# A new order, bank plan, engine choice and transposition form for an RWKV-7 plus mixer kernel on one core

## The chip, the core and the metric

The kernel runs on one core of a Trainium2 chip. The core's engines work side by side, each through its own list of instructions in order: TensorE (PE, with its weight loads PEld), VectorE (DVE), ScalarE (ACT), GpSimd (POOL) and SyncE (SP), which here only issues DMAs. An instruction waits on semaphores for what it needs, and everything behind it on its engine waits with it. The metric is the device time of one execution in microseconds (us); the median of the runs counts.

## The reference

Two parts, one behind the other. The first is a recurrence over 768 tokens for 4 batches of 8 heads with 40 x 40 states; the second mixes its output `x` (768 x 320 in each batch) over tokens and channels.

```python
for t in range(S):
    y[:, :, t] = np.einsum('bhd,bhde->bhe', rt, state)
    Sa = np.einsum('bhde,bhe->bhd', state, at)
    state = state * wt[:, :, None, :] - np.einsum('bhd,bhe->bhde', Sa, bt) \
            + np.einsum('bhd,bhe->bhde', vt, kt)
...
theta = x @ w_theta
zr, zi = x * np.cos(theta), x * np.sin(theta)
y = w_tok_r @ zr + w_tok_i @ zi
u = x + y
out = u + np.maximum(u @ w_ch, 0.0)
```

## The kernel before

The tokens are cut into chunks of 128: six to a batch, 24 in all, numbered i = 0 to 23. In a chunk the recurrence is turned into matrix products; from chunk to chunk only a state (`gt`) is handed on.

For each chunk these steps are planned, each an entry with a fixed number, an engine and a list of what it reads and writes:

- SP loads w, k, b, a, v and r (lines 485 and 501; for the first 8 chunks two chunks at a time). Buffers are few, so a load waits until the last reader of its buffer is done, and the loads behind it on SP wait too.
- `prep`: ScalarE takes the logarithm of w (L529), TensorE sums it, ScalarE takes exponentials (L563, L570, L574); GpSimd multiplies k, b and a with them (`kb` and `ah`, L513) or casts inputs to bf16 (L519). TensorE transposes the results (L434, L443), ScalarE (L472) or VectorE (L476) takes them out of PSUM into `feat`, `kb`, `nuT` and so on.
- `scores` (L716): three products of chunk columns, and a fourth in `readout`. Their 128 x 1024 results are masked on the way out: by VectorE in one instruction (L724), or copied by ScalarE (L726) and then masked by GpSimd with a select (L728).
- `recurrence` (x0 L755 and L760, nu L772, gt L793) and `readout` (y L885 and L891), with short evictions on ScalarE (`nx` L766, `nu` L776) and VectorE (`xp` L898).
- `theta` and `sines`: x is transposed (xT), multiplied with w_theta (L850 for the third part of the contraction, L857 for the rest), and ScalarE takes sine and cosine (L923); GpSimd multiplies them with x into `z` (L513).
- `mix_row`: 12 products per chunk with blocks of w_tok (L945), six steps of two; each step needs the `z` of one chunk of the same batch. Then `up` = sum + x on VectorE (L955), its transposition (uT), the channel product with w_ch (L850, L857), `oo` on VectorE (L979) and the store by SP (L982).

The weights come by GpSimd's own queue: w_theta (numbers 52 and 51) and w_ch (53 and 54) in two pieces each (L992), w_tok in six blocks of rows, each with a real and an imaginary half (L1000). A block of w_tok is transposed by TensorE before use. Steps that the prediction names by number: 96 and 97 load the first block of w_tok, 98 transposes it; 305 and 304 load the fifth, 306 transposes it; 363 and 364 load the sixth, 365 transposes it; 400 is the first channel product; 488 is `kb` of chunk 8; 493 and 666 are the casts of r for chunks 8 and 12, 819 that of v for chunk 14.

What sets the order is written out by hand in five tables. `ORDER` lists all 1396 steps; each engine does its own steps in that order. `HOMES` gives each PSUM result one of 8 banks, or a pair of them; a result can't be written before the last reader of the bank's former content is done. `PICK` lists the steps that take their other form:

- a cast on GpSimd instead of ScalarE or the other way round, an eviction on VectorE instead of ScalarE or the other way round;
- scores evicted by ScalarE with a GpSimd select instead of VectorE alone;
- a transposition done whole instead of in halves. Halved, each 128 x 128 block is two transposes of 64 rows, with a pair of banks for the result; whole, it is one transpose of 128 rows, in one bank where it fits.

`WARM` puts filler products of a constant tile (L1048) in front of named steps, as (count, bank). `Plan.thin` drops waits that another wait already implies.

Of the kernel before, what the change touches and what calls it, by code (L numbers as in the profile page):

```python
# [252 lines left out]
def kernel(  # L253
# [800 lines left out]
    for o in plan.order():  # L1054
        if o.idx in WARM:
            fill(*WARM[o.idx])
# [40 lines left out]
```

## Time and profile before

| | |
|---|---|
| median of 3 runs | 200.23 us (198.94 to 202.12) |
| profiled execution | 200.51 us |
| its span, first to last instruction | 197.9 us |
| granted TensorE clock | 0.996 |
| TensorE matmul, instructions | 4064 |
| bytes moved by DMA | 30.96 MB |

The span is what the profile covers; the 2.6 us beyond it are around the program. A view of the profile names a group as line, engine, operation, what is written and read, and its count; L716 is line 716 of the kernel. Busy time of TensorE is modelled from pipelined matmuls, so start-to-start distances are the better price of one.

### The profile page before, as it was taken

The page shows a single profiled execution, that of the slowest core. Times are in us where ns is not written, and L with a number is a line of the kernel's source. Part 1 is how long each engine was busy: PE and PEld are TensorE (multiplying, and loading weights), DVE is VectorE, ACT ScalarE, POOL GpSimd, SP SyncE. Part 2 cuts the span into 40 slices and gives each one's busy share as a digit, 9 for nine tenths or more (in the row PEclk, how much of TensorE's full clock was granted, in tenths as well). Part 3 has the DMA queues.
Part 4 walks back from the last instruction along what each step waited for, and adds up shares of the span by engine and source line. Part 5 has one row for each costly group of instructions (what it writes and reads, how often), then busy time and mean ns, then how long its engine had stood idle before and what let it go on. Part 6 is the DMA issues. An engine that isn't in the chain of part 4 may idle for free.

```text
span 197.9 us, 9187 instructions
## 1 busy us (share of the span) xinstructions
PE 184.9 (93%) x4064; PEld 147.0 (74%) x4064; DVE 158.4 (80%) x263; ACT 161.6 (82%) x304; POOL 144.8 (73%) x173
## 2 busy tenths in 40 slices
PE   7689999999997999999889999999999999999992
PEld 7568789888885768696667778867877777876650
DVE  7689999999999898889779778698885875971451
ACT  3599999999998999996689889999989878865020
POOL 6245576695699889999938997799999579578000
PEclk9999999999999999999999999999999999999998
DMA  5999988996999989989989949897984201000332
GB/s 128 296 275 286 337 202 180 217 177 100 196 157 176 198 138 191 187 136 215 139 143 159 211 139 180 202 158 160 277 146 69 70 11 62 0 3 3 132 123 76
DMA packets 106806, 30.96 MB, mean 156 GB/s; under 512 B 94224, under 2 KB 106768, under 8 KB 106768
## 3 DMA queue, kind: packets, MB, share of 16 engines
q1 hardware_dynamic: 102416, 27.53, 64.6%
q0 software_dynamic: 4352, 2.86, 9.1%
q8 instruction: 31, 0.51, 1.0%
q14 instruction: 7, 0.06, 0.1%
HBM read 29.29 MB, written 3.93 MB: 168 GB/s over the span
## 4 chain that ended last, share of the span: by engine, by line
PE 56%; DMA 15%; POOL 12%; ACT 10%; issue 3%; DVE 1%; SPq 1%; POOLq 0%
PE ps L945 18%; PE ps L716 7%; PE ps L434 6%; PE ps L857 6%; PE ps L443 5%; POOL z L513 3%; DMA raw_v<-in_v_dram 3%; DMA wrow<-in_moe_w_tok_i_dram 3%; PE ps L891 3%; DMA wth<-in_moe_w_theta_dram 3%; DMA raw_w<-in_w_dram 3%; POOL kb L513 3%; DMA raw_r<-in_r_dram 3%; PE ps L850 2%; ACT feat L686 2%
## 5 line engine op out<-in xcount | busy, mean ns | idle before, releaser
L945 PE MATMUL ps<-z,wtok 128*128 128x320 bf16 x288 | 48.7, 299 | 0.0
L724 DVE TENSOR_TENSOR lam<-ps,mask_p 128x1024 bf16<-128x1024 f32 x33 | 40.1, 1219 | 4.8 <-PE ps L716 4.7
L513 POOL TENSOR_TENSOR z<-cs,xp 128x640 bf16<-128x640 f32 x22 | 30.6, 1406 | 3.0 <-ACT cs L923 3.0
L945 PEld LDWEIGHTS <-wtok 128*128 128x128 bf16 x288 | 24.7, 97 | 8.8
L513 POOL TENSOR_TENSOR kb<-raw_kb,ex 128x640 bf16<-128x640 f32 x16 | 22.9, 1433 | 1.4 <-ACT nu L776 1.3
L724 DVE TENSOR_TENSOR phi<-ps,mask_n 128x1024 bf16<-128x1024 f32 x16 | 19.4, 1219 | 4.3 <-PE ps L716 4.1
L716 PEld LDWEIGHTS <-feat 64*128 64x128 bf16 x576 | 17.5, 94 | 6.3 <-issue 3.0
L724 DVE TENSOR_TENSOR psi<-ps,mask_p 128x1024 bf16<-128x1024 f32 x17 | 20.7, 1219 | 0.5 <-PE ps L716 0.3
L728 POOL TENSOR_SCALAR_AFFINE_SELECT lam<-lam 128x1024 bf16<-128x1024 bf16 x15 | 16.4, 1095 | 5.7 <-ACT lam L726 5.7
L716 PE MATMUL ps<-feat 64*128 64x128 bf16 x384 | 18.3, 217 | 0.5 <-DVE feat L666 0.2
L979 DVE SCALAR_TENSOR_TENSOR oo<-ps,up 128x640 f32<-128x640 f32 x11 | 9.1, 823 | 10.7 <-PE ps L857 10.6
L513 POOL TENSOR_TENSOR ah<-raw_a,ex 128x320 bf16<-128x320 f32 x16 | 12.9, 808 | 5.1 <-ACT ex L570 5.0
L726 ACT ACTIVATE lam<-ps 128x1024 bf16<-128x1024 f32 x15 | 15.3, 1029 | 0.4 <-PE ps L716 0.4
L891 PE MATMUL ps<-kb,lam 128*128 128x40 bf16 x384 | 15.6, 180 | 0.0
L472 ACT COPY feat<-ps 128x1024 f32<-128x1024 f32 x14 | 14.3, 1020 | 0.9 <-PE ps L434 0.9
L472 ACT COPY uT<-ps 128x384 f32<-128x384 f32 (+1 forms) x12 | 5.5, 457 | 11.6 <-PE ps L434 11.2
L891 PEld LDWEIGHTS <-lam 128*128 128x128 bf16 x384 | 13.9, 96 | 0.9 <-issue 0.4
L686 ACT COPY rT<-ps 128x512 bf16<-128x512 bf16 x24 | 14.1, 615 | 0.1
L529 ACT ACTIVATE lw<-raw_w 128x320 bf16<-128x320 f32 x24 | 11.7, 488 | 2.1 <-DMA raw_w<-in_w_dram 2.1
L955 DVE TENSOR_TENSOR up<-ps,xp 128x640 bf16<-128x640 f32 x11 | 9.1, 824 | 4.7 <-PE ps L945 4.7
L776 ACT ACTIVATE nu<-ps 128x320 bf16<-128x320 f32 x24 | 11.0, 458 | 2.0 <-PE ps L772 1.9
L885 PE MATMUL ps<-gd,rT 128*128 128x80 bf16 x80 | 12.2, 197 | 0.5 <-ACT cs L923 0.5
(173 smaller groups left out, 555.5 us busy)
## 6 DMA issues: line engine op xcount, KB each, us to landing
raw_w<-in_w_dram SPq DMA_DIRECT2D x24, 160.0 KB, 4.6
raw_r<-in_r_dram SPq DMA_DIRECT2D x12, 320.0 KB, 5.4
out_dram<-oo SPq DMA_DIRECT2D x11, 320.0 KB, 2.8
raw_a<-in_a_dram SPq DMA_DIRECT2D x16, 160.0 KB, 4.7
raw_kb<-in_k_dram SPq DMA_DIRECT2D x16, 160.0 KB, 4.2
raw_v<-in_v_dram SPq DMA_DIRECT2D x16, 160.0 KB, 4.5
raw_kb<-in_b_dram SPq DMA_DIRECT2D x16, 160.0 KB, 4.9
raw_kb<-in_k_dram SPq DMA_DIRECT2D x4, 320.0 KB, 6.0
```

Source lines behind the costliest of these rows:

```text
L434: nc.tensor.transpose(out=dst[:, c, n * 64:n * 64 + 64], in_=block[rows(c)], identity=ident[rows(c), rows(c)])
L472: nc.scalar.copy(out=to, in_=source)
L513: pool = ("POOL", lambda: nc.gpsimd.tensor_tensor(out=dst, in0=in0, in1=in1, op=ALU.mult))
L686: add("ACT", "e" + nm, i + x, lambda x=x, dst=dst: nc.scalar.copy(out=dst.rearrange("p g (t q) -> p g t q", q=8), in_=source(x)), 592, [pr ...
L716: nc.tensor.matmul(t[:, q, g, :], lhsT=lhs[rows(q), g, :], rhs=rhs[rows(q), g, :], start=True, stop=True)
L724: add("DVE", kindm, i, lambda: nc.vector.tensor_tensor(out=flat, in0=whole(), in1=mask.to_broadcast([128, 2 * G, 128]), op=ALU.mult), 1217 ...
L726: 1217, [p], dkeys, alts=(("ACT", lambda: nc.scalar.mul(out=flat, in_=whole(), mul=sign)),))
L728: add(None, "sel", i, None, 0, dkeys, dkeys, alts=(("POOL", lambda: nc.gpsimd.affine_select(out=flat, in_=flat, pattern=[[0, 2 * G], [1, 1 ...
L857: nc.tensor.matmul(ps(pk)[:, c, 0:DM], lhsT=lhs[:, 3 * c + kt, :], rhs=wt[:, kt, :], start=False, stop=kt == 1, skip_group_check=True)
L885: nc.tensor.matmul(t[:, g * 80:g * 80 + 80], lhsT=rT[:, g, :], rhs=gd[:, 2 * g:2 * g + 2, :], start=True, stop=False, skip_group_check=True)
L891: nc.tensor.matmul(t[:, h * D:h * D + D], lhsT=lam[:, n, p, g, :], rhs=kb[:, n, h, 0:D], start=first and n == 0, stop=n == 1, skip_group_c ...
L945: nc.tensor.matmul(to, lhsT=wtok[t % NCH][:, c, s, :], rhs=z[:, c, s], start=s == 0 and c == 0, stop=s == NT - 1 and c == 1)
```

## The change

Only the five tables are replaced. No function is changed, and every step is still done once.

```diff
 ORDER = [
-    0, 13, 21, 22, 23, 3, 16, 14, 4, 17, 5, 6, 2, 29, 19, 24, 25, 15, 18, 20, 26, 55, 58, 59,
...
+    0, 13, 21, 23, 4, 14, 17, 22, 3, 16, 19, 5, 18, 6, 20, 24, 26, 25, 2, 29, 15, 55, 58, 60,
...
 HOMES = [
-    0, 1, 2, 0, 4, 5, 6, 4, 2, 0, 6, 7, 4, 2, 6, 0, 1, 7, 4, 2, 1, 6, 4, 5, 1, 0, 5, 6, 0, 4, 2,
...
+    0, 1, 2, 4, 1, 6, 0, 4, 6, 2, 0, 1, 4, 0, 6, 2, 6, 7, 4, 0, 2, 3, 4, 5, 6, 2, 3, 6, 2, 3, 4,
...
 PICK = [
-    16, 17, 27, 28, 29, 33, 35, 37, 45, 46, 64, 73, 74, 87, 89, 107, 114, 115, 117, 120, 122,
...
+    16, 27, 28, 29, 30, 33, 37, 45, 46, 64, 65, 73, 74, 87, 89, 90, 92, 93, 107, 114, 117, 120,
...
-WARM = {19: (13, 2), 20: (3, 4), 21: (27, 0), 30: (4, 6), 33: (1, 6), 41: (3, 5), 58: (3, 4), 131: (2, 6), 173: (4, 3), 373: (1, 7)}
+WARM = {19: (13, 2), 20: (3, 4), 21: (27, 0), 30: (1, 0), 33: (3, 1), 41: (2, 1), 44: (7, 6), 58: (3, 6), 583: (5, 6), 599: (2, 3)}
```

Counted by kind, the choice of form and engine changes as follows.

| steps | before | after |
|---|---|---|
| transpositions done whole | 70 | 64 |
| of these: xt / gd / tr (x, state, r) | 12 / 12 / 6 | 8 / 14 / 4 |
| score evictions on ScalarE with a GpSimd select | 30 | 33 |
| wide `feat` evictions on ScalarE / VectorE | 14 / 2 | 12 / 4 |
| `uT` evictions on ScalarE / VectorE | 12 / 1 | 8 / 5 |
| casts of b and v on ScalarE | 2 | 4 |
| filler products | 61 | 66 |

The order differs on all five engines. In SP's list, for example, the load of r for chunk 8 moves from 24th to 43rd, that of v for chunk 2 from 15th to 13th. In GpSimd's list the first three weight DMAs move from places 23 to 25 to places 33 to 35, and the five weight DMAs of the fifth and sixth block and of w_ch's second piece stand in one run, where before two casts stood ahead of them and a select between them:

```
before: 777 (kb of chunk 13), 666, 819, 305, 363, 672 (a select), 364, 304, 54
after:  777 (kb of chunk 13), 646 (gt), 778 (ah of chunk 13), 304, 364, 363, 305, 54, 819, 666
```

200 rows, old and new, of tables (HOMES, ORDER, PICK) are left out of this document.

## The prediction

> **What bounds the kernel now.** I read the busy shares first, then the table of ten-microsecond windows, then the chain of waits and the waits themselves, and last the timelines of TensorE and GpSimd at the places that these point to.
>
> ```profile
> span 197.9 us, 9187 instructions
> PE 184.9 (93%) x4064; PEld 147.0 (74%) x4064; DVE 158.4 (80%) x263; ACT 161.6 (82%) x304; POOL 144.8 (73%) x173
> ```
>
> No engine is full over the whole span, and the shares don't say which one to follow. The windows do (start and end in us, width, then busy time of PE, PEld, DVE, ACT, POOL, the granted clock, the DMA share and GB/s):
>
> ```profile
> 40.00:50.00 10.00, 9.87 (x227) 8.76 (x226) 10.00 (x15) 9.94 (x22) 6.84 (x8) 1.00 0.87 137
> 50.00:60.00 10.00, 9.96 (x284) 8.61 (x282) 9.72 (x15) 9.99 (x24) 8.59 (x11) 1.00 0.96 175
> 60.00:70.00 10.00, 7.91 (x221) 6.39 (x214) 8.74 (x13) 8.78 (x16) 8.50 (x11) 1.00 1.16 187
> 80.00:90.00 10.00, 10.00 (x264) 8.14 (x259) 8.49 (x9) 9.30 (x20) 9.67 (x13) 1.00 0.88 162
> 90.00:100.00 10.00, 8.03 (x199) 6.16 (x196) 7.93 (x12) 6.08 (x12) 8.55 (x8) 1.00 0.99 165
> 150.00:160.00 10.00, 10.00 (x243) 7.84 (x243) 7.14 (x11) 8.15 (x16) 7.99 (x10) 1.00 0.14 42
> 180.00:190.00 10.00, 10.00 (x94) 6.49 (x93) 2.95 (x4) 2.38 (x6) 2.75 (x2) 1.00 0.19 66
> ```
>
> There are three stages. Up to 60 us ScalarE and VectorE are full (9.9 and 10.0 of 10): TensorE's time there has no value of its own. From 80 us to the end TensorE is full and nothing else is, except in 90 to 100, where all engines lose time together. In 60 to 70 TensorE and ScalarE also lose 2.1 and 1.2 us together. So a changed order can win in the two holes, and in TensorE's work after 80 us.
>
> The chain of waits (start, duration, what) and the table of waits (total, times, longest) show what the holes are:
>
> ```profile
> 13.05 6.53 DMA raw_v<-in_v_dram
> ...
> 48.50 5.11 DMA raw_r<-in_r_dram
> 53.66 0.32 POOL r L519
> ...
> 58.31 5.69 DMA wth<-in_moe_w_theta_dram
> 64.05 0.72 PE ps L857 x4
> ...
> 88.11 6.33 DMA wrow<-in_moe_w_tok_i_dram
> 94.48 0.35 PE ps L434 x12
> ```
>
> ```profile
> POOL o L519 <- DMA raw_v<-in_v_dram: 5.3, 2, 3.0
> ...
> ACT cs L923 <- PE ps L857: 1.8, 3, 1.2
> ...
> PE ps L857 <- DMA wth<-in_moe_w_theta_dram: 1.4, 1, 1.4
> ...
> PE ps L850 <- DVE wtok L476: 1.0, 1, 1.0
> ...
> PE ps L434 <- DMA wrow<-in_moe_w_tok_i_dram: 0.8, 1, 0.8
> ```
>
> Both holes are weights whose DMA GpSimd issues late in its own queue: w_theta's second piece at 58.31 for the first theta product at 64.05, and a row block of w_tok at 88.11 for its transposition at 94.48. GpSimd's order, not the DMA's speed, set both.
>
> **The change part by part.** Nothing is computed differently. Five tables change; I put each operation's number beside its engine in both plans and compared.
>
> *The weights of the second hole.* GpSimd around it, in the timeline, and one line of the DMA issues (the last column is us to landing):
>
> ```profile
> 84.89 0.72 POOL L519 CAST r<-raw_r 128x640 bf16<-128x640 f32 x1
> 85.55 0.46 POOL L519 CAST v<-raw_v 128x320 bf16<-128x320 f32 x1
> 85.95 0.59 POOL L1000 DMA_DIRECT2D wrow<-in_moe_w_tok_i_dram  x1
> ...
> 87.07 1.11 POOL L728 TENSOR_SCALAR_AFFINE_SELECT psi<-psi 128x1024 bf16<-128x1024 bf16 x1
> ...
> 89.18 0.84 POOL L992 DMA_DIRECT2D wch<-in_moe_w_ch_dram  x1
> ```
>
> ```profile
> wch<-in_moe_w_ch_dram POOLq DMA_DIRECT2D x1, 80.0 KB, 10.2
> ```
>
> The new order issues these five weight DMAs in one run and puts the cast r (666), the cast v (819) and the select behind them. The pair for transposition 365 ends 0.72 + 0.46 + 1.11 = 2.3 us earlier, more than the 0.8 us that TensorE waited at 94.48, so that wait goes: -0.8. The last wait, 1.0 us before the channel product 400 at about 99.5, is put down to a VectorE eviction, but wch's second piece lands at 89.18 + 10.2 = 99.4 as well. Either way it goes: the piece is issued 2.3 us earlier, and the new TensorE order puts four other steps between transposition 306 and product 400. -1.0. What is late next: for 365 the margin is thin, since the new order reaches it about 1 us earlier; 0.5 us is left. ScalarE has room (6.08 of 10 in that window). Ends: 0 and -1.8 for the two.
>
> *The first hole.* w_theta's second piece (51) now has only kb, ah, kb, a select and ah ahead of it from kb 488 on; three casts have left that stretch, so it could come about 1.6 us earlier and end the 1.4 us wait. But ScalarE, just ahead of the sines, had 1.2 us of cover there (its own wait for that product), and its work ahead of the first sine grows by 0.8: one score eviction more (1.03), one cast more (0.73), four short evictions and casts more (0.4 to 0.7 each, 2.0), one wide eviction fewer (1.02), five nuT fewer (0.38 each). The rows:
>
> ```profile
> L726 ACT ACTIVATE lam<-ps 128x1024 bf16<-128x1024 f32 x15 | 15.3, 1029 | 0.4 <-PE ps L716 0.4
> L472 ACT COPY feat<-ps 128x1024 f32<-128x1024 f32 x14 | 14.3, 1020 | 0.9 <-PE ps L434 0.9
> ...
> L472 ACT COPY uT<-ps 128x384 f32<-128x384 f32 (+1 forms) x12 | 5.5, 457 | 11.6 <-PE ps L434 11.2
> ...
> L472 ACT COPY nuT<-ps 128x256 f32<-128x256 f32 x12 | 4.6, 383 | 0.5 <-PE ps L434 0.5
> ...
> L518 ACT CAST z<-raw_a 128x640 bf16<-128x640 f32 x1 | 0.7, 725 | 1.3 <-DMA raw_a<-in_a_dram 1.3
> ```
>
> The 0.8 is hidden under the 1.2, and the product's 1.4 buys nothing that ScalarE could use. I take 0, with -1.4 and +0.8 as ends.
>
> *The first three weight DMAs* (96, 52, 97) go from places 23 to 25 of GpSimd's operations to places 33 to 35, directly ahead of kb 488 and behind cast r 493. This is the risk.
>
> ```profile
> 37.31 0.76 POOL L1000 DMA_DIRECT2D wrow<-in_moe_w_tok_r_dram  x1
> ...
> 38.88 0.59 POOL L1000 DMA_DIRECT2D wrow<-in_moe_w_tok_i_dram  x1
> ...
> 50.50 1.43 POOL L513 TENSOR_TENSOR kb<-raw_kb,ex 128x640 bf16<-128x640 f32 x1 [1.27 <-ACT nu L776]
> ```
>
> They take 2.2 us (37.31 to 39.47). Whether kb 488 still starts at 50.50 depends on the load for r 493, which SP now issues 43rd instead of 24th. The 44th load of before is the chain's raw_r, issued at 48.50 and landed at 53.6. If the new one lands then, kb 488 starts at 53.6 + 0.7 + 2.2 = 56.5, 6.0 late. But 544 KB of weights (192 + 160 + 192) no longer pass in front of it, and 320 KB of loads fewer: at the 137 to 175 GB/s of the two windows, 4.9 to 6.3 us. That gives a landing at 47.3 to 48.7 and kb 488 at 50.2 to 51.6. I take +0.4; ends 0 (an earlier kb is excluded: ScalarE's work ahead of chunk 8's exponentials isn't less) and +6.0. Behind them on GpSimd wait kb, ah and all of chunk 8; the first transposition of w_tok (98) then needs weights issued at about 50.3, whose landing, some 6 us later, just meets its old start near 56.9.
>
> *TensorE's work.* The tail shows its prices:
>
> ```profile
> 182.71 0.43 PE L857 MATMUL ps<-wch,uT 128*128 128x320 bf16 x2
> 182.98 4.51 PE L945 MATMUL ps<-z,wtok 128*128 128x320 bf16 x32
> 187.42 0.35 PE L434 MATMUL ps<-ident,up 64*128 64x64 bf16 x12
> 187.70 0.72 PE L945 MATMUL ps<-z,wtok 128*128 128x320 bf16 x4
> 188.35 0.31 PE L850 MATMUL ps<-wch,uT 64*128 64x320 bf16 x2
> ```
>
> Two 320-column matmuls of the 128-row form followed by the same form take 0.27 (182.71 to 182.98), so 0.135 each; four followed by the 64-row form take 0.65 (187.70 to 188.35), not 0.54. A change of form costs about 0.10. [...] In the two orders I count 166 such changes before and 170 after: +0.4. Whole transpositions go from 70 to 64: weighted by blocks, 54 go to halves and 16 come back, net 38. Halved, six blocks take 0.28 with one change of form in it, so 0.18, or 0.03 a block; a whole block moves 128 columns where a product moves 320 in 0.135, so 0.054. 38 x 0.024 = -0.9. The fillers grow from 61 to 66, in front of waits. Net -0.5; part lies before 80 us, where it is worth nothing: I take -0.3, ends -0.5 and +0.4.
>
> *ScalarE after the first sine.* Over the whole kernel it gets three more score evictions (+3.1), two wide ones (-2.0) and four uT (-1.8) fewer, one w_tok eviction more (under a feat's 1.02, say +0.8), and short ones: about +2.2 in all, of which 1.4 lie after the first sine. VectorE gets the opposite. In 150 to 160 ScalarE is idle 1.8 of 10, so most of it is covered; TensorE waits in order for each eviction's bank, so not all. +0.7, ends 0 and +1.4. The stores and other moved loads on SP: nothing, as in 150 to 160 the DMA share is 0.14 and earlier stores queue only loads for chunks well ahead; without that cover, the 2 to 3 us that a store waits.
>
> Sum: -0.8 - 1.0 + 0 + 0.4 - 0.3 + 0.7 = -1.0. The profiled execution took 200.51 us (197.9 of span and 2.6 around it), 0.28 above the median of three runs (200.23; 198.94 to 202.12). 199.5 for such an execution, 199.2 against the median.
>
> **The rivals.**
>
> *Slower: GpSimd is held at cast r 493.* For it: the load's place, 19 later, and the chain's own link raw_r to POOL r at 53.66. Against it: the lighter DMA traffic. If kb 488 starts s late, the time is 199.2 - 0.4 + s, less up to 1.2 of ScalarE's cover ahead of the sines: 197.6 + s to 198.8 + s. From s = 2.6, kb 488 at 53.1 or later, it is slower than before; at s = 4 it is 201.6 to 202.8, at s = 6 203.6 to 204.8.
>
> *No gain: ScalarE takes it back.* If all of its 2.2 counts and the hole at 60 us gives nothing, 199.2 - 0.7 + 2.2 = 200.7. For it: 9.9 of 10 up to 60 us, and TensorE's in-order waits for banks; against it: 1.8 idle of 10 late. This is also the case that the plan doesn't do what it was searched for and waits only move: 200 to 201.5.
>
> *More: the first 20 us shorten.* The chain holds raw_v from 13.05 to 19.58; its load is now SP's 13th issue instead of its 15th. GpSimd's second wait for raw_v was 5.3 - 3.0 = 2.3 us; if all of it goes and counts, 199.2 - 2.3 = 196.9; with the 1.4 of the first hole, 195.5. Against it: ScalarE is full by then.
>
> **How the numbers follow.** Forecast 0.40 (198.2 to 200.2), held GpSimd 0.24 (200.2 to 204.8, most likely 202.2), no gain 0.14, more 0.17, both bad cases together, over 204.8, 0.05. The range leaves out the lowest 0.10 and the highest 0.10: 196.0 to 204.5. Two per cent, about what a measurement of this kernel can tell from no change with runs 1.6% apart, is 196.2 and 204.2. Faster by more than that is half of the case "more" and a little of the forecast's edge, 0.13; slower by more is the top third of the held case and the last one, with a little of the third, 0.16; within 0.71.
>
> **What would show it.** Right: no wait of TensorE for wrow or wch in 90 to 100 and that window near 9.5 for PE; kb 488 between 50 and 52; PE full from 80 on as before, sum of ScalarE's busy time near 164. Wrong: a GpSimd wait for raw_r of over 2 us near 50, or for ScalarE in the windows after 100 with PE below 9.5; a hole of TensorE for wrow near 57. The forecast falls most easily on waits that no row of before shows, since every bank and order is new.

## The result and the profile after

The new plan takes 197.64 us (median of 4 runs, 197.18 to 197.91), the kernel before 200.56 beside it (4 runs, 198.94 to 202.12): ratio 0.990, 95% interval 0.985 to 0.995. That is 1.0% or 2.0 us less, 1.0 to 3.0 by the interval. The ratio leaves out executions in a slower state of the chip and is the more cautious figure; the medians are 2.9 us apart. The forecast was 199.2, a gain of 1.0. The profiled execution took 197.73 us with a span of 196.0; before it was 200.51 and 197.9, so 1.9 of its 2.8 us lie in the span.

Busy shares of the new plan, from the page:

```profile
span 196.0 us, 9263 instructions
...
PE 183.9 (94%) x4104; PEld 145.8 (74%) x4104; DVE 156.9 (80%) x263; ACT 163.3 (83%) x306; POOL 146.7 (75%) x174
```

Its windows (start and end in us, width, busy time of PE, PEld, DVE, ACT, POOL, granted clock, DMA share, GB/s):

```profile
50.00:60.00 10.00, 8.33 (x228) 7.25 (x226) 8.51 (x14) 8.63 (x22) 8.08 (x10) 1.00 1.02 159
60.00:70.00 10.00, 8.91 (x231) 7.11 (x228) 10.00 (x11) 9.94 (x19) 9.58 (x12) 1.00 1.19 198
...
80.00:90.00 10.00, 10.00 (x239) 7.69 (x237) 8.45 (x12) 8.97 (x18) 10.00 (x14) 1.00 0.94 161
90.00:100.00 10.00, 9.47 (x259) 7.29 (x255) 7.55 (x12) 8.76 (x18) 8.44 (x9) 1.00 0.85 135
...
150.00:160.00 10.00, 10.00 (x262) 7.70 (x255) 8.27 (x14) 8.87 (x15) 9.41 (x12) 1.00 0.11 36
```

TensorE gains 1.44 us in 90 to 100 (8.03 before) and 1.00 in 60 to 70 (7.91), and loses 1.63 in 50 to 60 (9.96). So one hole has nearly closed, one has become smaller, and one has opened ten microseconds earlier. The table of waits names the new one:

```profile
PE ps L434 <- DMA wrow<-in_moe_w_tok_r_dram: 1.9, 2, 1.5
PE ps L434 <- POOL z L519: 1.4, 2, 1.2
```

Before, the weight waits were 1.4 us for w_theta and 0.8 for a w_tok row block; both are gone, and the new wait of 1.5 us is at the first w_tok transposition (98). The second row above belongs to the start, at 7 us of the span, where the two plans lose about the same in all (6.5 and 6.6 us in the table below). GpSimd's timeline around it, and then TensorE's:

```profile
48.39 0.72 POOL L519 CAST r<-raw_r 128x640 bf16<-128x640 f32 x1
49.05 0.76 POOL L1000 DMA_DIRECT2D wrow<-in_moe_w_tok_i_dram  x1
49.80 0.85 POOL L992 DMA_DIRECT2D wth<-in_moe_w_theta_dram  x1
50.62 0.60 POOL L1000 DMA_DIRECT2D wrow<-in_moe_w_tok_r_dram  x1
51.19 1.49 POOL L513 TENSOR_TENSOR kb<-raw_kb,ex 128x640 bf16<-128x640 f32 x1
...
56.55 0.79 POOL L992 DMA_DIRECT2D wth<-in_moe_w_theta_dram  x1
...
87.87 0.78 POOL L519 CAST r<-raw_r 128x640 bf16<-128x640 f32 x1
```

```profile
59.16 0.52 PE L434 MATMUL ps<-ident,wrow 64*128 64x64 bf16 x24 [1.53 <-DMA wrow<-in_moe_w_tok_r_dram]
...
63.63 0.72 PE L857 MATMUL ps<-wth,xT 128*128 128x320 bf16 x4
...
92.70 0.53 PE L434 MATMUL ps<-ident,wrow 64*128 64x64 bf16 x24
```

Cast r 493 ran at 48.39, so its load came when the forecast had it, and kb 488 started at 51.19, 0.7 late. But the pair issued by 50.62 landed only at 59.1, as the chain of waits has it, and TensorE stood for 1.53 us:

```profile
50.62 8.49 DMA wrow<-in_moe_w_tok_r_dram
```

The theta product then starts without a wait (63.63, before 64.05), and 365, at 92.70, without one too.

To compare runs, TensorE's waits are counted by stretch: the time from one landmark's start to the next, less the work between them. The work is priced from start-to-start times of undisturbed rows (0.272 us for a pair of row products, 0.0295 for a halved block, 0.0556 for a whole one, 0.095 for a change of form); it sums to 177.2 us before and 177.0 after. The prices are those of the full clock, so what a lower granted clock costs is counted as waiting. Landmarks are the first products of the recurrence (x0) of chunks 8, 12 and 14 and the first theta product. All runs below are in the table:

| TensorE's waits, us, one profiled execution each | start to x0 of 6 | to x0 of 8 | to theta | to x0 of 12 | to x0 of 14 | to the last channel product | span |
|---|---|---|---|---|---|---|---|
| before | 6.5 | 0.5 | 1.7 | 1.9 | 2.5 | 1.1 | 197.9 |
| b1, weights in one run, old plan | 6.1 | 1.0 | 1.5 | 5.6 | 0.1 | 1.1 | 198.9 |
| b2, the same behind cast r 666 | 6.6 | 3.6 | 0.9 | 3.2 | 0.4 | 1.1 | 199.5 |
| b3, w_theta piece early, old plan | 6.2 | 1.4 | 0.3 | 2.6 | 2.1 | 1.1 | 197.4 |
| b4, first weights late, old plan | 6.5 | 3.4 | 0.1 | 2.4 | 2.1 | 1.1 | 199.3 |
| new plan | 6.6 | 1.8 | 0.4 | 1.9 | 0.9 | 1.2 | 196.0 |
| new plan again | 6.8 | 2.7 | 0.4 | 1.7 | 1.2 | 1.2 | 197.2 |
| a1, weights apart | 6.6 | 0.9 | 0.4 | 1.7 | 1.4 | 1.2 | 195.4 |
| a2, first weights early | 7.4 | 3.8 | 0.4 | 2.2 | 1.3 | 1.2 | 199.6 |
| a3, w_tok pair earlier | 6.9 | 0.2 | 3.6 | 2.1 | 1.2 | 1.2 | 198.6 |
| a4, both runs reordered | 6.3 | 0.2 | 4.1 | 2.5 | 0.2 | 1.2 | 198.0 |
| a5, pair earlier, w_theta kept | 6.7 | 0.2 | 0.4 | 2.4 | 0.5 | 1.2 | 194.7 |
| more changes of form | 6.6 | 1.3 | 0.4 | 2.1 | 0.5 | 3.7 | 199.6 |
| engines of before | 11.6 | 2.0 | 1.4 | 4.3 | 6.5 | 18.9 | 228.0 |

The column "to x0 of 8" varies between profiles where nothing ahead of it differs: 1.8, 2.7, 0.9 and 1.3 in the new plan (itself, again, a1, more changes of form), and 0.5, 1.0 and 3.6 in the old one (itself, b1, b2). The others stay within some 0.8 us where the plan is the same.

### The profile page after: what moved, and what is told of

Same layout as the page of the kernel before. It is cut to its first block, busy times and chain, and to the rows that moved or that the text cites. A ratio compares the mean times of both kernels' runs of the same rounds, so it can differ in the third digit from the quotient of the medians.

```text
span 196.0 us, 9263 instructions
## 1 busy us (share of the span) xinstructions
PE 183.9 (94%) x4104; PEld 145.8 (74%) x4104; DVE 156.9 (80%) x263; ACT 163.3 (83%) x306; POOL 146.7 (75%) x174
## 4 chain that ended last, share of the span: by engine, by line
PE 55%; DMA 14%; ACT 12%; POOL 9%; SPq 4%; DVE 3%; issue 2%; POOLq 0%
PE ps L945 17%; DMA wrow<-in_moe_w_tok_r_dram 11%; PE ps L434 7%; PE ps L716 7%; PE ps L857 5%; PE ps L443 4%; DMA raw_kb<-in_k_dram 3%; SPq L501 3%; PE ps L891 3%; POOL z L513 2%; ACT cs L923 2%; ACT lam L726 2%; PE ps L772 2%; PE ps L793 2%; POOL kb L513 1%
## 5 line engine op out<-in xcount | busy, mean ns | idle before, releaser
L945 PE MATMUL ps<-z,wtok 128*128 128x320 bf16 x288 | 47.1, 300 | 0.0
L724 DVE TENSOR_TENSOR lam<-ps,mask_p 128x1024 bf16<-128x1024 f32 x29 | 35.2, 1220 | 9.1 <-PE ps L716 8.9
L728 POOL TENSOR_SCALAR_AFFINE_SELECT lam<-lam 128x1024 bf16<-128x1024 bf16 x19 | 20.7, 1095 | 7.4 <-ACT lam L726 7.3
L724 DVE TENSOR_TENSOR psi<-ps,mask_p 128x1024 bf16<-128x1024 f32 x18 | 21.8, 1218 | 0.4 <-PE ps L716 0.4
L726 ACT ACTIVATE lam<-ps 128x1024 bf16<-128x1024 f32 x19 | 19.7, 1041 | 0.7 <-PE ps L716 0.4
L472 ACT COPY feat<-ps 128x1024 f32<-128x1024 f32 x12 | 12.2, 1016 | 1.1 <-PE ps L434 0.9
L728 POOL TENSOR_SCALAR_AFFINE_SELECT phi<-phi 128x1024 bf16<-128x1024 bf16 x8 | 8.7, 1093 | 5.2 <-ACT phi L726 5.2
L472 ACT COPY uT<-ps 128x384 f32<-128x384 f32 (+1 forms) x8 | 3.5, 443 | 10.4 <-PE ps L443 6.3
```

The lines of the kernel that those rows point to most:

```text
L472: nc.scalar.copy(out=to, in_=source)
L724: add("DVE", kindm, i, lambda: nc.vector.tensor_tensor(out=flat, in0=whole(), in1=mask.to_broadcast([128, 2 * G, 128]), op=ALU.mult), 1217 ...
L726: 1217, [p], dkeys, alts=(("ACT", lambda: nc.scalar.mul(out=flat, in_=whole(), mul=sign)),))
L728: add(None, "sel", i, None, 0, dkeys, dkeys, alts=(("POOL", lambda: nc.gpsimd.affine_select(out=flat, in_=flat, pattern=[[0, 2 * G], [1, 1 ...
L945: nc.tensor.matmul(to, lhsT=wtok[t % NCH][:, c, s, :], rhs=z[:, c, s], start=s == 0 and c == 0, stop=s == NT - 1 and c == 1)
```

## The experiments

Ratios are to the kernel before, run beside each experiment, and differences in us are worked out from the ratios. Steps are named by their numbers in GpSimd's own order.

**The new plan again**, as the partner of the next three.

> The changed kernel once more, to stand beside the others. All theories: 1.0% under the kernel before (ratio 0.985 to 0.995), span near 196, TensorE waiting about 1.5 us for wrow near 57 to 59 and not at all for wch.

198.66 us against 200.77, ratio 0.990 (0.985 to 0.994). The gain is there again, at the same size.

**b1: the second hole's weights in one run, alone, in the kernel before.**

```diff
-777, 666, 819, 305, 363, 672, 364, 304, 54, 701
+777, 304, 305, 364, 363, 54, 666, 819, 672, 701
```

> The kernel before, with only the five weight DMAs (304, 305, 364, 363, 54) put ahead of the casts 666 and 819 on GpSimd and in one run. Theory 'holes' (the gain is waits of TensorE that end): the waits of 0.8 and 1.0 us between 93 and 100 shrink by at least half, and the span gets 1.2 to 1.8 us shorter than before, ratio 0.991 to 0.994. Rival 'forms' (the gain is the new choice of engines and transposition forms, and the waits would be made up for later): under 0.5 us.

201.44 us, ratio 1.007 (1.002 to 1.012): slower. The wait for weights is gone (2.5 to 0.1 in the column "to x0 of 14"), but 3.7 us come in the one ahead of it. GpSimd's timeline and TensorE's row there:

```profile
84.62 0.59 POOL L1000 DMA_DIRECT2D wrow<-in_moe_w_tok_r_dram  x1
...
86.77 0.87 POOL L992 DMA_DIRECT2D wch<-in_moe_w_ch_dram  x1
87.57 0.78 POOL L519 CAST r<-raw_r 128x640 bf16<-128x640 f32 x1
```

```profile
88.41 1.04 PE L443 MATMUL ps<-ident,r 128*128 128x128 bf16 x8 [1.91 <-POOL r L519]
```

The five issues hold GpSimd from 84.62 to 87.57, and cast r 666 behind them is needed at once. Of the 3.7 us, 1.9 are this wait. Behind it the granted clock is at 0.50 for 3.4 us, by estimate worth up to 1.7 more (half of the 3.4); one of its windows (start and end, width, busy PE, PEld, DVE, ACT, POOL, clock, DMA share, GB/s):

```profile
89.00:90.00 1.00, 1.00 (x11) 0.82 (x8) 0.00 (x0) 0.52 (x2) 1.00 (x2) 0.50 1.29 224
```

In the old plan the transposition behind the cast (667) stands well ahead of 365 on TensorE; in the new one it stands directly ahead of 365, and there the cast can wait (87.87, the last row of the timeline above).

**b2: the same with cast r 666 left ahead of the run.**

```diff
-777, 666, 819, 305, 363, 672, 364, 304, 54, 701
+777, 666, 304, 305, 364, 363, 54, 819, 672, 701
```

> The kernel before, with GpSimd's cast r of chunk 12 left where it is and the five weight DMAs (304, 305, 364, 363, 54) in one run right behind it; the cast v of chunk 14 and the select come behind them. Theory 'the holes are worth their length': the weights come about 0.5 to 2 us earlier, TensorE's waits of 0.8 us for wrow and 1.0 us ahead of channel product 400 go, and nothing that is delayed is needed soon; 0.8 to 1.8 us faster than before, and the wait that the kernel of the first test showed at the transposition of r of chunk 12 (5.59 us in that stretch) is not there. Theory 'GpSimd's order is worth nothing without TensorE's': something else of the run's five late steps is waited for in the same stretch, and the time stays within 0.5 us of before.

199.64 us against 200.74, ratio 0.994 (0.989 to 0.999): 1.2 us faster, between both theories. The windows of 90 to 100 have TensorE at 9.19 (8.03 before), and 2.1 us of wait have left its column; 1.3 of them come back in the one ahead, where a select that the run delays is now waited for:

```profile
90.00:100.00 10.00, 9.19 (x210) 7.21 (x209) 8.12 (x10) 7.09 (x16) 8.38 (x10) 1.00 1.00 177
```

```profile
PE ps L760 <- POOL psi L728: 0.8, 1, 0.8
```

Its profiled execution took 201.16 us and its span of 199.5 shows no gain, because this execution lost 3 us elsewhere: TensorE waited 2.1 us for ScalarE, which waited for a load of w. Nothing was edited ahead of that place.

```profile
53.11 0.47 ACT L529 ACTIVATE lw<-raw_w 128x320 bf16<-128x320 f32 x1 [2.08 <-DMA raw_w<-in_w_dram]
```

**a1: in the new plan, the same weights apart again**, behind the casts.

```diff
-778, 304, 364, 363, 305, 54, 819, 666, 633, 784
+778, 666, 819, 305, 363, 633, 364, 304, 54, 784
```

> The changed kernel, with the five weight DMAs back behind the casts 666 and 819 and split by a select. 'Holes': TensorE waits again for wrow and wch between 92 and 100, 1.5 to 2.0 us in all, and the span is that much longer than the changed kernel's. 'Forms': no more than 0.5 us longer.

198.67 us, ratio 0.993 (0.989 to 0.997), 0.3% or 0.6 us behind the new plan, with overlapping intervals. One of the expected waits came, for the row block of 365, and none for w_ch:

```profile
PE ps L434 <- DMA wrow<-in_moe_w_tok_i_dram: 0.9, 1, 0.9
```

The column "to x0 of 14" is 1.4, against 0.9 and 1.2 in the new plan's two profiles, not 1.5 to 2.0 us more. So the theory 'holes' failed here: in the new plan the run's place on GpSimd is worth 0.2 to 0.5 us in the trace, and the time does not tell that from nothing.

**a2: in the new plan, the first three weight DMAs as early as GpSimd is free.**

```diff
-228, 254, 279
+228, 254, 97, 52, 96, 279
...
-493, 97, 52, 96, 488
+493, 488
```

> The changed kernel, with the first three weight DMAs (97, 52, 96) moved ahead into GpSimd's idle time near 39.4, behind select 254. 'Holes': the 1.5 us wait of TensorE for wrow at 57 to 59 goes, the first theta product comes 1.0 to 1.5 us earlier, and the span is 0.8 to 1.5 us shorter than the changed kernel's. Rival 'traffic' (544 KB at 39 to 44 delay the loads of r and k that chunk 8 waits for by some 3 us): cast r 493 starts after 50, kb 488 after 52, and the time is the same or up to 2 us longer.

201.25 us, ratio 1.006 (1.002 to 1.009): 1.6% slower than the new plan. GpSimd's timeline:

```profile
40.35 0.77 POOL L1000 DMA_DIRECT2D wrow<-in_moe_w_tok_i_dram  x1
...
51.36 0.45 POOL L519 CAST v<-raw_v 128x320 bf16<-128x320 f32 x1 [3.83 <-DMA raw_v<-in_v_dram]
...
52.80 0.72 POOL L519 CAST r<-raw_r 128x640 bf16<-128x640 f32 x1
53.48 1.43 POOL L513 TENSOR_TENSOR kb<-raw_kb,ex 128x640 bf16<-128x640 f32 x1
```

With 464 KB of weights in front, a load of v holds GpSimd for 3.83 us; cast r 493 comes 4.4 us later and kb 488 2.3 us later than in the new plan. (The prediction and the expectation count 544, with 160 for the first piece of w_theta. The DMA issues of before have 80 for it:)

```profile
wth<-in_moe_w_theta_dram POOLq DMA_DIRECT2D x1, 80.0 KB, 7.7
```

Idle time of GpSimd was no free place for its DMAs here: loads of SP came later behind them. The cast of v that waits ran at 51.36 instead of 46.50 in the new plan, and ScalarE waited 3.7 us in all for loads of w instead of 1.4.

**b4: the first three weight DMAs late, alone, in the kernel before.**

```diff
-178, 96, 52, 97, 313
+178, 313
...
-301, 488
+301, 97, 52, 96, 488
```

> The kernel before with the first three weight DMAs (97, 52, 96) directly ahead of kb of chunk 8, as late as in the new plan, everything else as it was. The prediction's step 'first weights late cost 0.4 us' (kb of chunk 8 0.4 to 1 us later, weights just in time): 0 to 0.8 us slower than before. Rival 'late weights cost TensorE's wait at the first w_tok transposition': the wait there is 1.5 us or more and the kernel 1.0 to 2.0 us slower. Rival 'less traffic in front of the loads helps as it did in the new plan': 0.5 to 1.5 us faster than before.

200.97 us against 200.64, ratio 1.005 (1.001 to 1.009): 1.0 us slower. kb 488 went from 50.5 to 51.2, as the step had it, but TensorE found its row block missing:

```profile
58.43 0.73 PE L434 MATMUL ps<-ident,wrow 64*128 64x64 bf16 x24 [1.69 <-DMA wrow<-in_moe_w_tok_r_dram]
```

This is the wait of the new plan (1.53 there), made by that edit alone. The interval takes in the forecast's 0.4 and reaches to 1.8.

**b3: w_theta's second piece earlier, alone, in the kernel before.**

```diff
-534, 576, 533, 51, 535
+534, 51, 576, 533, 535
```

> The kernel before, with the DMA of w_theta's second piece (51) ahead of the cast v of chunk 10 and kb of chunk 9 on GpSimd, right behind ah of chunk 9: issued near 56.6 instead of 58.3. The prediction's step 'TensorE's wait of 1.4 us at the first theta product buys nothing, because ScalarE has 1.2 us of cover': within 0.4 us of before, with TensorE waiting as long later in 60 to 70. Rival 'the first hole counts as TensorE's time': the theta product 1.4 us earlier and the kernel 0.8 to 1.4 us faster. Second rival, as the tests with earlier weights showed: kb of chunk 9, now 0.8 us later, is waited for, and it is 0 to 0.8 us slower.

200.15 us against 200.74, ratio 0.997 (0.992 to 1.001). The wait of TensorE for w_theta is gone, and so is ScalarE's for that product: three waits of 1.8 us, the longest 1.2, became two of 0.6:

```profile
ACT cs L923 <- PE ps L857: 0.6, 2, 0.3
```

The hole is gone (1.7 to 0.3), and about 0.7 us of time, which the interval does not tell from nothing; it holds both the prediction's 0 and the rival's lower end of 0.8. In this profile 0.9 of the 1.4 reappear ahead of it, in the column that varies from run to run. The profile also names the wait ahead of the channel product 400 (L850 with w_ch), which that of before puts down to VectorE:

```profile
PE ps L850 <- DMA wch<-in_moe_w_ch_dram: 1.2, 1, 1.2
```

**a3: in the new plan, the first w_tok pair ahead of cast r 493**, and w_theta's first piece (52) directly ahead of its second.

```diff
-341, 493, 97, 52, 96, 488
+341, 97, 96, 493, 488
...
-534, 51
+534, 52, 51
```

> The new kernel with the first w_tok pair (97, 96) ahead of the cast r of chunk 8 (493) instead of behind it, and w_theta's first piece (52) right ahead of its second (51), so that the first w_tok transposition (98) has its weights 1.5 us earlier and kb of chunk 8 starts 0.8 us earlier or at the same time. Theory 'the 1.5 us wait of TensorE for wrow at 98 is GpSimd's place, and counts': that wait falls under 0.5 us, 0.5 to 1.5 us faster than the new plan. Theory 'traffic': the loads of chunk 8 and 9 are delayed as much as the weights come earlier, and the time is the new plan's within 0.5 us. Theory 'the hole only moves': the wait at 98 goes, and the first theta product (368) waits for w_theta instead; within 0.5 us.

199.84 us, ratio 0.999 (0.995 to 1.004): the gain is gone. The wait at 98 fell as expected (column "to x0 of 8": 0.2), and the hole moved as the third theory said, but grew on the way (3.6 us in the next column), as the first piece of w_theta is now late:

```profile
PE ps L850 <- DMA wth<-in_moe_w_theta_dram: 2.3, 1, 2.3
...
PE ps L857 <- DMA wth<-in_moe_w_theta_dram: 0.8, 1, 0.8
```

**a4: a3, and in the later run the pair for 365 first.**

```diff
-778, 304, 364, 363, 305, 54
+778, 364, 363, 304, 305, 54
```

> The kernel of the test before this one, and in the later run of five weight DMAs the pair of the transposition that comes first on TensorE (364 and 363 for 365) ahead of 304 and 305. Theory 'waits for wrow count where TensorE is full': the wait ahead of 365 (1 to 1.6 us in that stretch) falls under 0.5 us, and it is 0.5 to 1.2 us faster than the test before this one. Theory 'the next wait takes its place': 306, whose pair now comes last, or VectorE's evictions wait instead, and the gain is under 0.4 us.

200.06 us, ratio 0.997 (0.994 to 1.001), no different from a3, though the column "to x0 of 14" falls from 1.2 to 0.2 in its profile and the span from 198.6 to 198.0. A gain of this size was not separated from the spread.

**a5: the pair ahead of cast r, w_theta's first piece behind it, and the later run as in a4.**

```diff
-341, 493, 97, 52, 96, 488
+341, 97, 96, 493, 52, 488
...
-778, 304, 364, 363, 305, 54
+778, 364, 363, 304, 305, 54
```

> The new kernel with the first w_tok pair (97, 96) ahead of the cast r of chunk 8 and w_theta's first piece (52) behind it, ahead of kb of chunk 8 (at its place of the new plan or 0.8 us earlier than there), and in the later run 364 and 363 ahead of 304 and 305. Theory 'both remaining weight waits count': TensorE's wait at the first w_tok transposition falls from 0.9-2.7 us to under 0.5 and does not come back at the first theta product, the stretch with 365 waits under 0.4 us; 1 to 2.5 us faster than the new plan, which makes it the fastest. Theory 'the transfers set it': 320 KB of weights ahead delay loads or the second w_theta piece by as much, and the time is within 0.6 us of the new plan.

197.14 us against 200.64, ratio 0.985 (0.980 to 0.990), the fastest of all. Both weight waits are gone; the column "to x0 of 12" is 0.5 us longer than the new plan's (2.4 and 1.9), with a wait of 1.2 that the profile does not name. Its windows, beside those of the new plan above:

```profile
50.00:60.00 10.00, 9.86 (x289) 8.81 (x291) 10.00 (x15) 9.99 (x26) 9.65 (x11) 1.00 0.98 159
...
90.00:100.00 10.00, 9.73 (x252) 7.57 (x251) 8.64 (x12) 9.10 (x16) 9.34 (x9) 1.00 0.84 133
```

It beats the kernel before by 1.5% (1.0 to 2.0). Against the new plan's 1.0% it is 0.5% better with overlapping intervals; its six executions were not run beside the new plan, so that part is likely, not shown.

**Engines of before in the new plan.** All choices between ScalarE, VectorE and GpSimd go back (44 and 35 steps of `PICK`), order, banks (`HOMES`) and transposition forms stay.

```diff
-    16, 27, 28, 29, 30, 33, 37, 45, 46, 64, 65, 73, 74, 87, 89, 90, 92, 93, 107, 114, 117, 120,
+    16, 17, 27, 28, 29, 30, 33, 37, 45, 46, 64, 73, 74, 87, 89, 107, 114, 115, 117, 120, 122,
...
```

> The new kernel with every choice between ScalarE, VectorE and GpSimd as the kernel before had it (44 steps and 35 go back); order, banks and TensorE's transposition forms stay the new ones. The prediction's step 'the new choices load ScalarE by 2.2 us more and cost 0.7': ScalarE's busy time falls by about 1.7 us, and it is 0.7 us faster than the new plan or the same. Rival 'the choices fit this order': 1 to 2 us slower, with new waits of TensorE for evictions after 60 us. Third: under 0.5 us either way, the balance hardly matters.

228.42 us against 200.64, ratio 1.142 (1.137 to 1.147): 28 us slower than before and 30 slower than the new plan, far outside every theory. The page, and the first of TensorE's waits:

```profile
PE 190.6 (84%) x4104; PEld 149.0 (65%) x4104; DVE 158.9 (70%) x263; ACT 163.2 (72%) x304; POOL 145.2 (64%) x173
```

```profile
PE ps L760 <- POOL psi L728: 3.6, 2, 2.8
PE ps L716 <- ACT feat L472: 3.4, 3, 1.3
...
PE ps L716 <- ACT nuT L472: 1.5, 2, 1.3
...
PE ps L716 <- DVE kb L476: 1.4, 2, 1.2
```

No engine has over 2 us more to do: ScalarE is busy 163.2 us (163.3 in the new plan), VectorE 158.9 (156.9), GpSimd 145.2 (146.7). The time went into waits of TensorE for results of all three, 18.9 us of them behind chunk 14, where the new plan has 1.2. The sum of an engine's work says nothing here. What counts is likely whether each result's engine is free when the order and the banks want it; the two were not tried apart.

**More changes of form.** Ten row products are moved between two steps of the 64-row form, so TensorE changes its form 190 times instead of 170. One of the ten:

```diff
-    973, 735, 736, 737, 738, 974, 991, 996, 1168, 441, 924, 923, 1126, 920, 975, 935, 992, 1109,
-    961, 994, 943, 739, 740, 741, 742, 743, 1106, 944, 962, 1142, 960, 976, 1108, 957, 1107,
+    973, 735, 736, 737, 974, 991, 996, 1168, 441, 924, 923, 1126, 920, 975, 935, 992, 1109, 961,
+    738, 994, 943, 739, 740, 741, 742, 743, 1106, 944, 962, 1142, 960, 976, 1108, 957, 1107,
```

> The new kernel with ten row products moved between two steps of the 64-row form, so that TensorE changes its form 190 times instead of 170, all of the added ones where it is full. The prediction's price of 0.10 us a change, all of it on the path: 2.0 us slower than the new plan. [...] Rival 'changes are covered by other work or cost nothing': under 0.5 us.

202.37 us, ratio 1.008 (1.004 to 1.012): 1.8% or 3.6 us slower than the new plan. The place of this edit in its timeline, and then the same place of the new plan:

```profile
124.20 0.40 PE L716 MATMUL ps<-rT,feat 64*128 64x128 bf16 x8
124.53 0.45 PE L945 MATMUL ps<-z,wtok 128*128 128x320 bf16 x2
124.91 0.41 PE L434 MATMUL ps<-ident,kb 64*128 64x64 bf16 x16
```

```profile
125.24 0.40 PE L716 MATMUL ps<-rT,feat 64*128 64x128 bf16 x8
125.47 0.40 PE L434 MATMUL ps<-ident,kb 64*128 64x64 bf16 x16
```

The scores take 0.33 us to the next start in place of 0.23, the pair of products 0.38 in place of the 0.27 of the prediction's tail: 0.10 and 0.11 for each change. Through eight of the ten places TensorE takes 0.20 to 0.24 us longer, again 0.10 to 0.12 a change. Through the other two it takes 1.2 and 0.4 us longer, and 0.8 are lost behind the second of these; the waits view has most of this:

```profile
PE ps L434 <- DVE up L955: 1.5, 2, 0.9
```

`up` is the sum that a block of row products completes, and a moved product makes it late. The price of 0.10 on the path is right; the rest is not form but order.

## Why the prediction was right, and where not

The stated range, 196.0 to 204.5, held, and the time is within two per cent of before, the case with 0.71. But 197.64 lies below the 198.2 to 200.2 of the case that was called the forecast, in the part left to "More", whose mechanism did not come. The sum was 1.0 short, and that it was no further off is in part luck: its terms were wrong in both directions.

**The second hole, -1.8.** Right in the result, its mechanism only half. The column "to x0 of 14" falls from 2.5 to between 0.5 and 1.3 in the five runs with the new plan there (itself, again, a2, a3, more changes of form); TensorE is at 9.47 in 90 to 100, and no wait for wrow or wch stands there, as the markers said. But "GpSimd's order, not the DMA's speed, set both" was taken to mean that its order alone would do. b1 is slower than before; b2 brings 1.2; and with the weights back behind the casts in the new plan (a1) the column is still 1.4, so about 1.1 of the 1.6 us do not hang on GpSimd's order. TensorE's new order is the likely reason: it has five steps between 306 and 400, where the old one had none. It was not tried by itself. Of the two readings of the wait ahead of 400, b3 speaks for w_ch's landing. In the old plan the price of the earlier run lay with cast r 666, which the prediction moved behind the run and costed at nothing, without asking who waits for it. By the two orders it was free in the new plan because TensorE's order moved 667 too. The select 672, which the prediction also has behind the run, is not there: VectorE masks those scores in the new plan.

**The first hole, 0.** The net is near the forecast, but not for its reason. The piece was issued at 56.55 (58.31 before), 1.8 us earlier where 1.6 was expected, and TensorE's wait fell by 1.3 (1.7 to 0.4). But 1.3 us of new wait for the first weights stand in the column ahead of it, and the two columns make 2.2 us in both plans. They are not independent: in b4, where w_theta's second piece was not touched, this column falls from 1.7 to 0.1, because TensorE comes later. The reason given was ScalarE's cover; it was real and went too (b3: 1.2 to at most 0.3), so it did not absorb what the piece gained. TensorE has hardly any spare time from 80 us on (in the new plan busy 10.00, 9.47 and 9.99 of 10 in the three windows from 80 to 110), so its own lost time in the hole likely counts, which is not shown: b3, with that edit alone, measured 0.7 us (0.2 slower to 1.5 faster), and a5, with 0.6 us left in the two columns, is the fastest kernel.

**The first weights, +0.4.** The feared mechanism, GpSimd held at cast r 493, did not come: cast at 48.39, kb 488 at 51.19, in the ranges given. (With 464 KB in place of 544 the working gives kb 488 at 50.8 to 52.0, which holds it as well.) But the sentence that the weights' landing "just meets" the first w_tok transposition was the place that failed: "some 6 us" were 8.5 in the profile, TensorE stood for 1.5, and the forecast's own sign of error, a hole for wrow near 57, is there. Alone it costs 1.0 us (b4; 0.2 to 1.8). a2 shows the price of the other extreme: weights issued from 40.35 on instead of 49.05 hold up the loads and make the kernel 1.6% slower. A place just ahead of the cast (a5) is likely the best of the three.

**TensorE's work, -0.3.** The price of 0.10 for a change of form, which decides it, is measured again by the added changes. By prices the work falls by 0.2 from 177.2 to 177.0; the busy time falls from 184.9 to 183.9, but that figure is modelled. The price of whole against halved transpositions was not tried by itself.

**ScalarE after the first sine, +0.7.** This step was wrong in kind. ScalarE's busy time is near the forecast (163.3, "near 164"), but TensorE's waits behind chunk 14 are 1.2 against 1.1: none of it showed. With nearly the same sum of work and the old choices in the new order and banks the kernel is 28 us slower than before. Load was the wrong measure; that single steps' places on their engines are the reason for the 28 us fits the waits, but was not shown step by step.

**The rivals.** "Held GpSimd" and "no gain" did not come. "More" gave 195.5 to 196.9 by a shorter start; the start is the same (x0 of chunk 6 at 47.7 and 48.0). What separates the sum from the result is mainly its two losses, +0.4 and +0.7: by the table the first stretch came out even, and ScalarE's price was not paid.

By the table the waits fall by 1.4 us in all (-1.6 second hole, -1.3 first, +1.3 first weights, +0.2 the rest) and work by 0.2: 1.6 of the span's 1.9.

## What to carry to other kernels

A weight DMA's place had three prices here: who waits for it (1.5 us of TensorE in the new plan, 1.7 in b4), who waits for what is moved behind it on the issuing queue (1.9 us for cast r 666 in b1), and which loads its bytes delay (3.83 us of GpSimd for a load of v in a2); a change that fixed one in isolation lost by another (b1 made its plan 1.4 us slower, a2 3.2, a3 1.9), so take each step that is displaced and look up its reader's place. Two waits of TensorE that follow each other can be one term: in b4 the first grew from 0.5 to 3.4 us and the second, though w_theta's second piece was not moved, fell from 1.7 to 0.1, so add them up before either is priced. A wait well ahead of the stretch where TensorE is full likely still counts, even where a full engine seems to cover it (b3 0.7 us faster, with an interval that holds 0; a5, with 0.6 us left of such waits, the fastest at 0.985). Choices of engine belong to the order and bank plan they were made for (30 us between two sets of them in the new order, with busy sums no more than 2.0 us apart): don't price them by an engine's sum of busy time, and don't carry them over unmeasured.

## What the hardware showed that was not expected

In a4 a hole of TensorE cost more than its length. The wait of 2.75 us for w_theta is followed by a granted clock of 0.50; the windows of one microsecond (same columns as above) and the rows of the theta product:

```profile
62.00:63.00 1.00, 0.00 (x0) 0.00 (x0) 1.00 (x2) 1.00 (x1) 1.00 (x2) 1.00 1.16 197
63.00:64.00 1.00, 0.00 (x0) 0.00 (x0) 0.29 (x1) 0.13 (x1) 0.98 (x3) 0.69 1.20 196
...
66.00:67.00 1.00, 1.00 (x8) 0.37 (x8) 0.00 (x0) 0.01 (x1) 0.00 (x0) 0.50 1.30 228
...
70.00:71.00 1.00, 1.00 (x23) 0.75 (x21) 1.00 (x2) 0.99 (x2) 1.00 (x1) 0.90 0.16 26
```

```profile
64.56 0.45 PE L850 MATMUL ps<-wth,xT 64*128 64x320 bf16 x2 [2.75 <-DMA wth<-in_moe_w_theta_dram]
65.73 1.23 PE L857 MATMUL ps<-wth,xT 128*128 128x320 bf16 x4 [0.72 <-DMA wth<-in_moe_w_theta_dram]
```

The four products take 1.23 us where the new plan's take 0.72, and the clock stays at half from 63.4 to 70.2, for 6.8 us. The same, for 3.4 us each, follows the wait of 1.91 in b1 (its transposition of r), that of 2.1 in b2 and that of 1.69 in b4, but not that of 2.4 in the new plan's second profile, whose windows from 58 to 64 us all have 1.00. Over 12 executions each, the mean granted clock is 0.982 in a3 and a4, 0.993 in the new plan; in 93 executions of the kernel before, the 38 with a clock of 0.995 or more have a median of 199.9 us and the 7 below 0.985 one of 202.3. So part of the spread between runs of one kernel goes with the clock. It is not only behind such holes that the clock falls: in three profiles (new plan again, a2, a3) it is also at half for 3.4 us from 7.4 to 7.7 us on, in the start, which the new plan's own profile passes at full clock with the same steps. What makes it fall in one execution and not in another was not shown.
